# A pad of 384 bytes ahead of the SBUF tiles of a decode-attention kernel, so that rows loaded by DMA begin at multiples of 256 or 512 bytes

## Chip, cores, metric

One core of one Trainium2 chip. The time is device microseconds (us) of one execution. The kernel before takes 657.46 us (median of 5 runs, 657.27 to 658.13, which is 0.13%).

## The reference

One decode step of grouped-query attention with a large K and V cache, multiplied by a small MLP branch (the MLP is about 3 MB of weights and plays no part here). What matters is the size of the caches:

```python
B, Sq, D = 4, 1, 448
Hq, Hkv, Sk, Dh = 16, 8, 8192, 256          # k_cache, v_cache: (4, 8, 8192, 256) bf16
...
q = (xn @ wq)                                # one query row per batch and head
scores = einsum("bhqd,bhkd->bhqk", q, k) * Dh ** -0.5     # k, v repeated over 2 query heads
o = einsum("bhqk,bhkd->bhqd", softmax(scores), v)
s = o @ wo                                   # wo: (4096, 448)
return x + s * silu(mlp(xn))
```

There are 32 pairs (batch, kv head), here called heads. Each has 4 MB (4,096 KB) of K and as much of V, and each byte of them is read once. With the weights that makes 279 MB.

## The kernel before

All tiles are declared in one list, and they lie in SBUF in that order. Sizes are per partition:

```python
def sb(name, shape, dty):
    return es.enter_context(nc.sbuf_tensor(name, shape, dty))

kn = sb("kn", [P, 2, NCH, DH], BF16)         # 2 K slots of 32,768 B
vb = sb("vb", [P, 2, NCH, DH], BF16)         # 2 V slots of 32,768 B
kT = sb("kT", [P, RING, TB * P], BF16)       # 16,384 B
wo_sb = sb("wo_sb", [P, HQ, NHALF, D], BF16) # 16 rows of 1,792 B
...                                          # some 45 small tiles
```

In the built program 16,384 B of scratch and four constants of 32 B each lie ahead, so `kn` begins at byte 16,512 of each partition, `vb` at 82,048 and `wo_sb` at 163,968. Each of these is 128 B past a multiple of 256 (and of 512).

SP issues all large loads on one queue. Two K slots and two V slots are refilled as soon as compute has left them:

```python
def load_k(h):
    b, g = where(h)
    if h >= 2:
        sp.wait_ge(S["v_k"], h - 1)
    sp.dma_start(kn_dst(h), A_k_cache[b, g].rearrange("(p c) d -> p (c d)", p=P)
                 ).then_inc(S["dk%d" % (h % 2)], 16)
... # load_v alike; the last head's V in pieces
load_k(0)
load_k(1)
load_wo(NLATE, HQ, "dwo")                    # 12 rows of 1,792 B per partition
for h in range(2, NH):
    load_k(h)
    load_v(h - 2)
load_v(NH - 2)
load_v(NH - 1)
... # four late rows of wo
```

For each head PE transposes K (into PSUM), DVE and ACT copy it to `kT`, PE computes the scores, ACT the exponentials, and PE multiplies by V two heads later.

## Time and profile before

| | before |
|---|---|
| time, median of 5 runs | 657.46 us |
| span of the profiled run | 656.9 us |
| bytes moved by DMA | 279.13 MB |
| share of the span in which the main queue's packets occupy the 16 engines | 99.2% |
| PE idle, waiting for K, before the transposes | 76 us |

The page of the kernel before. The first two lines cut the span into 40 equal slices: how busy the DMA engines were, in tenths, and what they moved. Then come the totals and the DMA queues (packets, megabytes, share of 16 engines), and two issue lines (output<-source, count, KB each, median us from issue to landing):

```profile
...
DMA  8999999999999999999999999999999999999996
GB/s 360 440 413 425 434 427 437 425 439 427 437 427 435 429 435 431 431 435 427 437 429 433 429 433 429 433 429 433 429 435 431 433 431 435 429 433 433 429 425 256
DMA packets 12353, 279.13 MB, mean 425 GB/s; under 512 B 1204, under 2 KB 3256, under 8 KB 3768
## 3 DMA queue, kind: packets, MB, share of 16 engines
q1 hardware_dynamic: 12328, 278.99, 99.2%
...
kn<-in_A_k_cache_dram SPq DMA_DIRECT2D x32, 4096.0 KB, 25.7
vb<-in_A_v_cache_dram SPq DMA_DIRECT2D x31, 4096.0 KB, 31.3
```

The DMA is at 9 in every slice but the first and the last. A load of 4,096 KB moves in 9.7 us (8 packets on each engine, 1213.5 ns each), yet takes 25.7 us from issue to landing, so each stands behind another one in the queue. Now the waits of the same kernel (engine, tile and line; who ended the wait; us in total, times, longest), and the groups of the transposes and of the two evictions (busy us, mean ns of one, idle before and what ended it):

```profile
...
PE pst L588 <- PEq L245: 76.3, 28, 4.6
```

```profile
...
L588 PE MATMUL pst<-ident_b,kn 128*128 128x128 bf16 x4096 | 347.3, 239 | 78.6 <-PEq L245 76.3
L295 ACT ACTIVATE kT<-pst 128x1024 bf16<-128x1024 bf16 x224 | 229.3, 1024 | 360.6 <-ACTq L245 359.5
...
L293 DVE COPY kT<-pst 128x1024 bf16<-128x1024 bf16 x288 | 197.5, 691 | 263.7 <-DVEq L245 263.7
```

The first line is PE idle while K has not landed: 76.3 us in 28 waits. The two evictions stand idle before their input for 263.7 us (DVE) and 360.6 us (ACT). Compute has slack in every head; the DMA has none. So a nanosecond saved per packet should be saved in the time.

**Packets.** The trace also holds one record per DMA packet: start, duration, bytes. It does not name the engine, but they can be strung into 16 chains in which one packet follows the other without a gap (8,037 of the 8,064 packets of 32 KB have a successor within 40 ns of their bytes / 27.2), and the distance from one start to the next in a chain is what a packet costs. (These distances are worked out from the records, not lines of the profile. They were taken over whole ranges of packets and are good to a few hundredths of a ns in the mean. The duration in a record is 3 to 4 ns longer than the distance: 1213 against 1209.4 ns, 239 against 235.3, 469 against 465.9.) Times in the records' own clock run some 11 us ahead of the span's.

| packets, before | bytes / 27.2 | mean distance, first 50 us | mean distance, later |
|---|---|---|---|
| 32,768 B (K, V) | 1204.7 ns | 1209.8 ns | 1213.5 ns |
| 12,544 B (w3) | 461.2 | 465.9 | - |
| 6,272 B (w4) | 230.6 | 235.3 | - |
| 1,792 B (wo) | 65.9 | 70.6 | 75.3 |

At the start a packet of any of these four sizes costs its bytes at 27.2 B per ns plus 4.7 ns, both fitted to the distances (1209.4 less 235.3 ns for 32,768 less 6,272 B is 27.2 B per ns; 1209.8 and not 1209.4 for 32 KB, because two of the 16 engines already pay more in that stretch). Later it costs more for both sizes that occur later in number: 4.1 ns at 32,768 B (1213.5 less 1209.4) and 4.7 at 1,792 B (75.3 less 70.6). The 75.3 ns are those of the early wo load from 52 us of the records' clock on; the wo rows at the very end took 72.8.

### The profile page before, as it was taken

How to read it: one execution, taken by the hardware profiler on the slowest of the kernel's cores; microseconds unless marked ns; L12 is line 12 of the kernel's file. 1: busy time of each engine (PE TensorE's matmuls, PEld its weight loads, DVE VectorE, ACT ScalarE, POOL GpSimd, SP SyncE). 2: the span in 40 equal slices, each digit the busy share in tenths (PEclk: the TensorE clock that was granted, in tenths of full speed). 3: DMA queues.
4: the chain of work that ended last, by engine and by line, in shares of the span. 5: the costliest groups of instructions: out<-in, count | busy, mean ns of one | idle time of the engine just before them, and what ended most of it. 6: DMA issues, size and time to landing. Idle time of an engine off the chain costs nothing. (4 is left out here: it accounts for less than half of the span.)

```text
span 656.9 us, 22864 instructions
## 1 busy us (share of the span) xinstructions
PE 556.3 (85%) x9937; PEld 476.3 (73%) x9937; DVE 276.5 (42%) x589; ACT 256.0 (39%) x364; POOL 13.4 (2%) x77
## 2 busy tenths in 40 slices
PE   1899997988888988888897888898888889888897
PEld 0487886876766887667787766798767678766775
DVE  7353554443443444434443443444334443433442
ACT  4144544442433443323444333444333344433340
POOL 2000000000000000000000000000000000000000
PEclk9698999887899878889987888988878987887998
DMA  8999999999999999999999999999999999999996
GB/s 360 440 413 425 434 427 437 425 439 427 437 427 435 429 435 431 431 435 427 437 429 433 429 433 429 433 429 433 429 435 431 433 431 435 429 433 433 429 425 256
DMA packets 12353, 279.13 MB, mean 425 GB/s; under 512 B 1204, under 2 KB 3256, under 8 KB 3768
## 3 DMA queue, kind: packets, MB, share of 16 engines
q1 hardware_dynamic: 12328, 278.99, 99.2%
q8 instruction: 7, 0.11, 0.1%
q14 instruction: 2, 0.02, 0.0%
q10 hardware_dynamic: 16, 0.01, 0.0%
HBM read 278.99 MB, written 0.00 MB: 425 GB/s over the span
## 5 line engine op out<-in xcount | busy, mean ns | idle before, releaser
L588 PE MATMUL pst<-ident_b,kn 128*128 128x128 bf16 x4096 | 347.3, 239 | 78.6 <-PEq L245 76.3
L295 ACT ACTIVATE kT<-pst 128x1024 bf16<-128x1024 bf16 x224 | 229.3, 1024 | 360.6 <-ACTq L245 359.5
L588 PEld LDWEIGHTS pst<-ident_b,kn 128*128 128x128 bf16 x4096 | 275.4, 108 | 84.3 <-issue 83.8
L293 DVE COPY kT<-pst 128x1024 bf16<-128x1024 bf16 x288 | 197.5, 691 | 263.7 <-DVEq L245 263.7
L600 PE MATMUL psc<-qc,kT 128*128 128x2 bf16 x4096 | 178.7, 165 | 0.0
L600 PEld LDWEIGHTS psc<-qc,kT 128*128 128x128 bf16 x4096 | 157.7, 98 | 28.5 <-issue 28.3
L639 PE MATMUL psv<-vb,pT 128*4 128x512 bf16 x1056 | 86.4, 378 | 0.3 <-issue 0.3
L618 PE MATMUL psm<-sel,po 128*128 128x2 f32 x272 | 36.8, 257 | 0.5 <-PEq L245 0.5
L618 PEld LDWEIGHTS psm<-sel,po 128*128 128x128 f32 x272 | 34.8, 197 | 0.9 <-issue 0.9
L639 PEld LDWEIGHTS psv<-vb,pT 128*4 128x4 bf16 x1056 | 22.3, 82 | 15.3 <-issue 0.8
L452 DVE TENSOR_REDUCE rmax<-psc 128x2 f32<-128x128 f32 x32 | 9.3, 292 | 48.8 <-DVEq L245 48.8
L470 DVE COPY po<-psv 128x512 f32<-128x512 f32 x34 | 23.5, 692 | 3.0 <-DVEq L245 2.3
L457 DVE TENSOR_REDUCE gmax<-psm 2x1 f32<-2x128 f32 x32 | 8.9, 279 | 34.7 <-DVEq L245 34.7
L317 ACT ACTIVATE pT<-psc,negb 128x64 bf16<-128x64 f32 x66 | 20.6, 331 | 5.4 <-ACTq L245 5.4
L612 PEld LDWEIGHTS psm<-diag,ones_f 2*128 2x128 f32 x66 | 14.1, 263 | 6.4 <-issue 5.4
L280 POOL COPY qc<-qT 128x4 bf16<-128x4 bf16 x32 | 5.9, 186 | 585.8 <-DVEq L469 568.6
L612 PE MATMUL psm<-diag,ones_f 2*128 2x2 f32 x66 | 16.8, 321 | 1.1 <-PEq L245 0.9
L317 ACT ACTIVATION_READ_ACCUMULATOR pT<-psc,negb 128x1 f32 x66 | 13.6, 206 | 0.0
L608 PEld LDWEIGHTS psm<-ident_f,rmax 128*2 128x2 f32 x32 | 2.6, 80 | 14.0 <-issue 14.0
L536 PE MATMUL pst<-ident_b,xn_b 4*128 4x4 bf16 x14 | 0.6, 161 | 13.6 <-DVE xn_b L365 8.9
L630 PE MATMUL psm<-rowsum,ones_f 128*128 128x2 f32 x64 | 11.6, 251 | 0.0
L536 PEld LDWEIGHTS pst<-ident_b,xn_b 4*128 4x128 bf16 x14 | 0.5, 100 | 13.6 <-issue 8.9
(101 smaller groups left out, 122.4 us busy)
## 6 DMA issues: line engine op xcount, KB each, us to landing
kn<-in_A_k_cache_dram SPq DMA_DIRECT2D x32, 4096.0 KB, 25.7
vb<-in_A_v_cache_dram SPq DMA_DIRECT2D x31, 4096.0 KB, 31.3
vb<-in_A_wq_dram SPq DMA_DIRECT2D x1, 3584.0 KB, 11.7
vb<-in_B_w_dram SPq DMA_DIRECT2D x2, 1568.0 KB, 16.6
wo_sb<-in_A_wo_dram SPq DMA_DIRECT2D x1, 2688.0 KB, 44.3
kn<-in_A_v_cache_dram SPq DMA_DIRECT2D x1, 2048.0 KB, 25.2
kn<-in_A_v_cache_dram SPq DMA_DIRECT2D x1, 1024.0 KB, 27.3
kn<-in_A_v_cache_dram SPq DMA_DIRECT2D x2, 512.0 KB, 28.5
```

The source lines that it names most:

```text
L293: engine.tensor_copy(dst, src).then_inc(S["v_ev"], 1)
L295: engine.activation(dst, src, ACT.Copy).then_inc(S["a_ev"], 1)
L317: ins = act.activation(pv_p[:, :, hh], sc[:, :, hh], ACT.Exp, bias=negb[:, s, hh:hh + 1], scale=SCALE, accum_out=rowsum[:, s, hh:hh + 1])
L452: v.tensor_reduce(rmax[:, :], psc[h % 2][:, 0:NCH * REP].rearrange("p (k h) -> p h k", h=REP), AX.X, ALU.max).then_inc(S["v_rmax"], 1)
L457: v.tensor_reduce(gmax[:, :], psm[0:REP, 0:P], AX.X, ALU.max).then_inc(S["v_s"], 1)
L470: v.tensor_copy(po[:, slot], psv[:, 0:CP * DH]).then_inc(S["v_po"], 1)
L588: ins = pe.transpose(dst[:, t * P:(t + 1) * P], kn[:, h % 2, GC * j + kl, half * P:(half + 1) * P], ident_b[:, :])
L600: ins = pe.matmul(psc[h % 2][:, kk * REP:(kk + 1) * REP], kT[:, j % RING, t * P:(t + 1) * P], qc[:, h % 2, half, :], start=(half == 0), st ...
L612: pe.matmul(psm[:, P:P + REP], ones_f[0:REP, :], diag[:, :], start=True, stop=True).then_inc(S["p_m2"], 1)
L618: ins = pe.matmul(dst(dh)[:, 0:width], po[:, slot, i * DH + dh:(i + 1) * DH:NHALF], sel[:, i, 0:width], start=(i == 0), stop=(i == CP - 1))
L630: pe.matmul(psm[:, P + REP:P + 2 * REP], ones_f[:, :], rowsum[:, h % 2, :], start=True, stop=True)
L639: ins = pe.matmul(psv[o:o + CP * REP, 0:CP * DH], pT[:, h % 2, kk * REP:(kk + CP) * REP], src[:, kk:kk + CP, :].rearrange("p c d -> p (c d)"),
```

## The change

Its intent: bring the starts of the rows that the DMA writes to multiples of 256 or 512 B. It adds a tile that nothing reads or writes. The whole diff:

```diff
     NWARM = 14
+    ROW_PAD = 192
...
+        align = sb("align", [P, ROW_PAD], BF16)
         kn = sb("kn", [P, 2, NCH, DH], BF16)
         vb = sb("vb", [P, 2, NCH, DH], BF16)
```

192 elements of bf16 are 384 B. `kn` moves to byte 16,896 (33 x 512), `vb` to 82,432 (161 x 512) and `wo_sb` to 164,352 (321 x 512). K and V rows are 32,768 B, so all of them begin at multiples of 512; wo rows are 1,792 B (7 x 256), so they begin at multiples of 256.

## The prediction

Parts are cut from it where marked, because no trace or run of this case shows what they say. One is an argument that put the 4.7 ns of every packet down to its start off the boundary: 697 packets x 4.7 ns, 3.3 us in all. "That reading" in the text is this one; the prediction itself dropped it. So the 3.3 us is not in the sum, which came to 656.6 us, 0.9 below the 657.46 of before, for the chance of 2 to 3 us.

> **What bounds the kernel now.** The DMA engines. The slice table shows DMA 9 (90% or more) in all but the first and last of 40 slices, at 413 to 440 GB/s; the queue table gives 278.99 MB and 99.2% of 16 engines' time on one queue. In the waits, PE idles 76 us of 657 before the K transposes, while a K load takes 25.7 us from issue to landing although its 4 MB move in 9.7 us: a load always stands queued behind another. Compute has slack in every head, the DMA none. After the last weight piece some 6 us remain (chain of waits: last output matmuls 2.42 us, two DVE steps of 0.4 us, the store).
>
> **What one packet costs.** From the packet records of the trace, followed engine by engine: at the start a 32,768 B packet takes 1209.4 ns, a 12,544 B one 465.9, a 6,272 B one 235.3, a 1,792 B one 70.6. All fit bytes / 27.2 B per ns plus 4.7 ns[...]. From about 51 us on, the mean rises to 1213.5 ns (fixed part 8.8) and for 1,792 B to 75.3 (9.4). With some 697 data packets per engine the fixed parts sum to about 6 us; the bytes take 641 us.
>
> **What the change does.** It adds no instruction, byte or packet. By the declarations the first tile begins 128 B past a multiple of 512; the pad brings K and V rows (32,768 B) to multiples of 512 and wo rows (1,792 B) to multiples of 256.[...]
>
> **Does this trace agree?** Only by half. 4.7 ns is the fixed part, but w4 argues against that reading: of its two runs per partition one lands 128 B off a 256 B boundary and the other on a multiple of 512, and all 256 packets took 239 ns in the record (235.3 ns apart). So I take the fixed 4.7 ns to be independent of alignment. I can't exclude that the extra 4 ns per packet after 51 us is an alignment cost under contention; removing it would give, by estimate, 500 x 4.1 = 2 us. Removing every fixed cost would give 6 us, under 1%. Engines should be indifferent: all tiles move by the same 384 B (transposes 219 ns median, DVE evictions 691, ACT 1024).
>
> **Prediction.** 656.6 us, 8 times in 10 between 654.0 and 658.0. Faster by over 2%: 1%; within 2%: 98%; slower by over 2%: 1%. The likeliest outcome is no measurable change; the centre is pulled down by the chance of 2 to 3 us.
>
> **What would show each step.** Packets and bytes unchanged. Spacing of 32 KB packets in steady state: 1213.5 ns if alignment does nothing, 1209.4 if the later extra is alignment; at the start 1204.7 if the fixed part is. The w4 packets, whose two runs swap alignment, still 235.3 ns. Steady slices near 431 GB/s, or 433 to 435. PE's wait before the K transposes near 76 us, unless loads get faster.
>
> **What would make it wrong.** Compute reads of SBUF colliding with DMA writes in a way that depends on the offset[...].

## The result

655.51 us (median of 5 runs, 654.8 to 655.92) against 657.46: 1.95 us less. The ratio is 0.9963, 95% interval 0.9951 to 0.9975. A ratio here is made from all fast runs of both kernels, so it is not quite the ratio of the medians quoted. That is well within 2%, but the interval excludes 1.

The lines of the page after that answer to those shown of before:

```profile
...
DMA  8999999999999999999999999999999999999996
GB/s 362 444 421 421 443 421 446 421 444 423 444 423 444 421 446 421 446 421 446 421 443 423 442 425 442 425 442 425 438 429 438 429 438 429 434 434 434 434 424 288
DMA packets 12354, 279.13 MB, mean 427 GB/s; under 512 B 1205, under 2 KB 3257, under 8 KB 3769
## 3 DMA queue, kind: packets, MB, share of 16 engines
q1 hardware_dynamic: 12328, 278.99, 99.3%
...
kn<-in_A_k_cache_dram SPq DMA_DIRECT2D x32, 4096.0 KB, 25.2
vb<-in_A_v_cache_dram SPq DMA_DIRECT2D x31, 4096.0 KB, 30.5
```

```profile
...
PE pst L590 <- PEq L247: 76.0, 28, 4.5
```

```profile
...
L590 PE MATMUL pst<-ident_b,kn 128*128 128x128 bf16 x4096 | 345.8, 238 | 77.8 <-PEq L247 76.0
L297 ACT ACTIVATE kT<-pst 128x1024 bf16<-128x1024 bf16 x224 | 229.5, 1025 | 357.6 <-ACTq L247 356.7
...
L295 DVE COPY kT<-pst 128x1024 bf16<-128x1024 bf16 x288 | 197.5, 692 | 260.9 <-DVEq L247 260.9
```

Packets and bytes are the same (one packet more is an instruction fetch, on a different queue: q14 has 3 instead of 2). The DMA is as full as before, the mean rate went from 425 to 427 GB/s, and a K load lands in 25.2 us instead of 25.7. PE's wait for K is unchanged (76.0 us), and the groups that work in every head changed by at most 3 ns per instruction. What changed is in the packets:

| mean distance of packets | before | after | less per engine, over the whole run |
|---|---|---|---|
| 32,768 B, 8,064 of them | 1213.34 ns | 1209.41 ns | 1.98 us |
| 1,792 B, 2,043 counted | 73.50 | 70.45 | 0.39 |
| 4,096, 8,192 and 16,384 B (last head's V) | - | each 3.3 to 4.0 ns less | 0.12 |
| 28,672, 12,544, 6,272 B (first weights) | - | unchanged | 0.00 |

The last column is the difference times the number of packets over 16 engines. It sums to 2.5 us, where the medians differ by 1.95 and the ratio says 2.4. After the change, 8,049 of 8,064 K and V packets have the same recorded duration, 1213 ns; before nearly all lay between 1213 and 1228, spread. So the whole gain is the later extra, which is gone, and the 4.7 ns that every packet costs from the start is still there.

The two profiled runs differ by 3.8 us in their spans (656.9 and 653.1), more than the timed runs do. Part of that is luck at the end. The chain that ended last, before and after, in order of time (start us, us, what):

```profile
...
651.61 2.42 PE pst L687 x24
```

```profile
...
648.76 1.52 PE pst L689 x24
```

The same 24 last matmuls took 2.42 us in one run and 1.52 in the other. A windows line gives the stretch, each engine's busy us and instructions (PE, weight loads, DVE, ACT, POOL), the granted clock, the DMA share and GB/s; before and after:

```profile
...
651.00:654.50 3.50, 2.52 (x29) 1.95 (x25) 0.59 (x3) 0.00 (x0) 0.00 (x0) 0.60 0.08 31
```

```profile
...
648.00:651.00 3.00, 2.04 (x42) 1.49 (x41) 0.84 (x3) 0.00 (x0) 0.00 (x0) 1.00 0.15 55
```

The granted clock was 0.60 in the first and 1.00 in the second. That 0.9 us goes with the clock and not with the change: in the profiled run of `wo_late`, an experiment below that has the tiles at the old addresses, the same 24 matmuls took 1.43 us at a granted clock of 1.00, and in that of `pad352`, again off the boundary, 2.44 at 0.51. The line of `wo_late`:

```profile
...
660.79 1.43 PE pst L687 x24
```

### The profile page after: what moved, and what is told of

Its sections match the earlier page's. It is cut to its first block, busy times and chain, and to the rows that moved or that the text cites. A ratio compares the mean times of both kernels' runs of the same rounds, so it can differ in the third digit from the quotient of the medians.

```text
span 653.1 us, 22864 instructions
## 1 busy us (share of the span) xinstructions
PE 552.8 (85%) x9937; PEld 473.5 (73%) x9937; DVE 276.1 (42%) x589; ACT 256.2 (39%) x364; POOL 13.5 (2%) x77
## 6 DMA issues: line engine op xcount, KB each, us to landing
kn<-in_A_k_cache_dram SPq DMA_DIRECT2D x32, 4096.0 KB, 25.2
vb<-in_A_v_cache_dram SPq DMA_DIRECT2D x31, 4096.0 KB, 30.5
```

## The experiments

Theory A: a packet whose SBUF start is not on a 256 B boundary pays for itself. Rivals, as they came up: 512 B is the boundary; the move itself matters; the cost grows with the bytes below the start; short packets, compute, or other engines start the extra.

Every kernel gave the correct result except `bare`, `engines`, `onset` and `mix`, which load only and return zeros. `src_off` reads shifted K, yet its result was still within the tolerance of the comparison. "Distance" is the mean distance of 32 KB packets, in the kernels between 130 and 640 us of the records' clock.

### pad256, pad128, pad352, pad160: other sizes of the pad

```diff
-    ROW_PAD = 192
+    ROW_PAD = 128      # pad256; 64 in pad128, 176 in pad352, 80 in pad160
```

> Pad of 256 B: every tile moves, but K, V and wo rows begin 128 B past a multiple of 256 again, as before. Theory A (start against the 256 B boundary): as before, late 32 KB packets 1213.5 ns apart, time ratio to before 0.999 to 1.001. Rival D (it is the move, or having a pad, whatever its size): 1209.4 ns and a ratio of 0.996 to 0.997.

> Pad of 128 B: K and V rows begin 256 B past a multiple of 512, wo rows at multiples of 256. Theory A (256 B is the boundary): 1209.4 ns, ratio 0.996 to 0.997. Rival B (512 B is the boundary): an extra remains for K and V, 1211 to 1213.5 ns, ratio 0.998 to 1.000.

In the next two, theory A is taken with a cost in proportion to the bytes below the start: 224 and 32 B where the kernel before has 128 B and 4.1 ns. A mechanism given for it, which no run shows, is cut.

> Pad of 352 B: rows begin 224 B past a multiple of 256. Theory A[...]: extra 7/4 of 4.1 ns, so about 1216.6 ns, ratio 1.002 to 1.004. Rival C (any start off the boundary costs the same): 1213.5 ns, ratio about 1.000.

> Pad of 160 B: rows begin 32 B past a multiple of 256. Theory A[...]: extra about 1 ns, 1210.4 ns, ratio about 0.997. Rival C (any start off the boundary costs the same): 1213.5 ns, ratio about 1.000.

| kernel | start past a multiple of 256 (of 512) | distance | median of 5 | ratio to before (95%) |
|---|---|---|---|---|
| before | 128 (128) | 1213.50 ns | 657.86 us (9 runs) | 1 |
| pad256 | 128 (384) | 1213.44 | 657.75 | 0.9998 (0.9985 to 1.0012) |
| pad128 | 0 (256) | 1209.42 | 655.32 | 0.9955 (0.9941 to 0.9968) |
| pad352 | 224 (480) | 1214.53 | 658.56 | 1.0008 (0.9994 to 1.0022) |
| pad160 | 32 (288) | 1214.53 | 658.3 | 1.0006 (0.9992 to 1.002) |

Of 256 and 512 B, 256 B is the boundary: pad128 gets all of the gain (1209.42 ns) with K and V at odd multiples of 256, so rival B falls, and pad256, which moves every tile but keeps the residue, gets none (1213.44 ns), so rival D falls. That the cost grows with the bytes below the start falls too: 224 B and 32 B past the boundary cost the same 5.1 ns (1214.53 less 1209.42), where one would have been seven times the other. Being off the boundary is what costs, with a small difference between 128 B (4.1 ns) and 32 or 224 B (5.1 ns). The time alone could not have told 32 and 128 apart; the packet records do.

### src_off: the reading side

```diff
+                at = (b * HKV + g) * SK * DH - (64 if h < NH - HKV else 0)
+                at = max(at, 0)
+                kf = A_k_cache.rearrange("b g s d -> (b g s d)")
-                sp.dma_start(kn_dst(h), A_k_cache[b, g].rearrange("(p c) d -> p (c d)", p=P)
+                sp.dma_start(kn_dst(h), kf[at:at + SK * DH].rearrange("(p n) -> p n", p=P)
```

> The kernel after the change, but K of heads 0 to 23 is read from 128 B earlier in DRAM (result wrong on purpose); heads 24 to 31 and all V are read from the boundary. If a start off 256 B costs on the reading side as well: K packets of heads 0 to 23 about 1213.5 ns or more, those of 24 to 31 1209.4 ns. If only the SBUF side counts: 1209.4 ns throughout.

1209.41 ns throughout, with K of heads 1 to 23 shifted as well as with heads 24 to 31 (head 0 is not shifted, because the address is held at 0), and 654.53 us in its single run. A start in DRAM 128 B off the boundary costs nothing that shows (1209.41 ns, as after the change); a start 128 B off in SBUF costs 4.1. (K loads alternate here with V loads that are on the boundary. The next run shows that such a mixture hides most of an extra, but on the SBUF side it still left 1209.95 ns; and `bare`, below, has six shifted loads in a row.)

### k_only: K on the boundary, V off it

```diff
         kn = sb("kn", [P, 2, NCH, DH], BF16)
+        gap = sb("gap", [P, 64], BF16)
         vb = sb("vb", [P, 2, NCH, DH], BF16)
```

> K rows at multiples of 512 as after the change, but a gap of 128 B between the K and V slots puts V (and wo) 128 B off the boundary, as before. Theory A (each misaligned packet pays for itself): K packets 1209.4 ns, V packets 1213.5 ns, half of the gain, ratio to before about 0.998. Rival E (misaligned packets put the engines into a state in which all packets pay): K packets too above 1209.4 ns, and more than half of the gain is lost.

Neither came. The mean over K and V was 1209.95 ns: not half of the extra but an eighth of it (0.54 of 4.1 ns). The median was 656.46 us (655.42 to 658.13), ratio 0.998 (0.9968 to 0.9993), which fits half of the gain as well as nearly all of it; the packets decide. Successive distances on one engine, from a V load (off the boundary) over a K load to a V load (a bar stands for the 4 B packet that ends a load):

```
V: 1209 1210 1209 1210 1209 1209 1216 1209 | K: 1209 1213 1210 1209 1210 1209 1209 1210 | V: 1209 1210 1209 1209 1210 1209 1213 1211 | K: 1216 1209 ...
```

In each V load the first six packets pay nothing, the next two begin to pay, and one or two packets into K it is over. So theory A as stated falls: a misaligned packet does not pay for itself at once. The distances behave as if a sum grew over misaligned packets (six free, the next two dearer by up to 7 ns) and shrank over aligned ones; what it is a sum of they do not show.

### wo_late: without the early run of short packets

```diff
-            load_wo(NLATE, HQ, "dwo")
             for h in range(2, NH):
                 load_k(h)
                 load_v(h - 2)
+            load_wo(NLATE, HQ, "dwo")
             load_v(NH - 2)
```

> The kernel before, without a pad, with the early wo load (the one with 1,792 B packets) moved behind the loads of all heads but the last two. Tells what starts the extra. Rival F (the run of many short packets starts it): K and V packets stay at 1209.4 ns until wo is loaded near the end, ratio 0.997. If something else starts it (compute, time, or the loads themselves): 1213.5 ns from about 51 us or a little later, ratio about 1.000.

The extra set in without wo: the mean distance per load rose from 1209.8 to 1213.2 ns between 65 and 114 us of the records' clock, engine by engine: ten of the 16 began to pay 38 to 48 packets after K2's load began, six within 15. Why those six were early is open; six instruction fetches of 16 KB lie between 41 and 79 us of that clock, but that they are the reason is not shown. Rival F falls. The time rose to 663.28 us (ratio 1.0079), for another reason: the wo load had filled a hole. K2 is issued at 42.7 us (before), when compute has left the first K slot, and without wo nothing is queued before that. Windows lines, columns as above; before and wo_late:

```profile
...
30.00:40.00 10.00, 10.00 (x189) 9.13 (x188) 4.29 (x8) 5.76 (x10) 0.00 (x0) 0.98 0.94 394
40.00:45.00 5.00, 5.00 (x109) 3.66 (x110) 2.39 (x5) 1.88 (x2) 0.00 (x0) 1.00 1.07 388
```

```profile
...
30.00:40.00 10.00, 10.00 (x185) 8.98 (x184) 4.11 (x7) 5.60 (x9) 0.00 (x0) 0.96 0.76 326
40.00:45.00 5.00, 5.00 (x114) 3.85 (x114) 2.53 (x7) 2.05 (x2) 0.00 (x0) 1.00 0.39 105
```

From 40 to 45 us the DMA moved 105 GB/s instead of 388, from 30 to 40 us 326 instead of 394: (394 - 326) x 10 + (388 - 105) x 5 is 2.1 MB less, at 427 GB/s by estimate 4.9 of the 5.4 us. (The profiled run of wo_late was its slowest, 666.64 us; the other five took 662.9 to 663.34.)

### bare: loads alone, many offsets in one run

All compute is taken out. SP issues 4 MB K loads into four slots, one after another, each waiting only for the load that last used its slot:

```python
PHASES = (("d128", 64, 0, 6), ("wo", 64, 0, 1), ("d128b", 64, 0, 6), ("d0", 0, 0, 6), ("d128c", 64, 0, 6),
          ("d32", 16, 0, 6), ("d64", 32, 0, 6), ("d224", 112, 0, 6), ("d0s128", 0, 64, 6),
          ("d128s128", 64, 64, 6), ("d0b", 0, 0, 6))       # name, SBUF offset, DRAM offset (elements), loads
```

> Only loads, no compute (result wrong on purpose): six 4 MB K loads each with the SBUF start 128 B off, then wo at 128 B off, then 128, 0, 128, 32, 64, 224 B off, then DRAM 128 B off with SBUF at 0 and at 128, then both at 0. Theory A (the extra is the DMA engines' own): after the onset the phases at 128 take 1213.5 ns, at 32 and 224 about 1214.6, at 0 1209.4. Rival G (it needs compute engines that use SBUF beside the DMA): 1209.4 ns in every phase. Rival F (short packets start it): 1209.4 in the first phase, 1213.5 in the one after wo.

| phase | distance per load, ns (pauses left out) |
|---|---|
| 128 B | 1209.6, then 1209.4 five times |
| wo, 128 B | (short packets) |
| 128 B | 1213.6, then 1213.3 to 1213.5 |
| 0 | 1210.1, then 1209.4 |
| 128 B | 1209.4 three times, 1209.7, 1212.6, 1213.5 |
| 32 B | 1214.3 to 1214.8 |
| 64 B | 1213.3 to 1213.7 |
| 224 B | 1215.2, then 1214.4 to 1214.8 |
| 0, DRAM 128 B off | 1209.6, then 1209.4 |
| 128 B, DRAM 128 B off | 1209.4 three times, 1209.6, 1213.1, 1213.3 |
| 0 | 1209.8, then 1209.4 |

A windows line of this run shows how empty the compute engines are; the columns are as above, for DVE and POOL, the only ones that have work in it:

```profile
...
100.00:300.00 200.00, 0.00 (x0) 0.00 (x0) 1.00 1.00 433
```

No engine ran a single instruction in 200 us and the extra has the same size as in the kernel (1213.3 to 1213.5 ns against 1213.50; aligned 1209.4 in both), so rival G falls. Misaligned loads after aligned ones are free for about four loads (1209.4 to 1209.7 ns), with or without a DRAM offset, and pay from then on (1212.6 to 1213.5). After the short packets the next phase pays at once (1213.6 ns), as it would if each packet, short or long, counted alike; but six free loads came before them too, so this phase doesn't prove that they hastened it.

### engines: is it contention among DMA engines?

```python
PHASES = ((128, 16, 4), (17, 16, 5), (128, 16, 2), (34, 16, 4), (128, 16, 2), (68, 16, 3), (119, 16, 3), (128, 16, 3), (17, 0, 2))
# rows, SBUF offset in elements (32 B), loads; all loads of a phase have landed before the next begins
```

> Only loads of 32 KB rows, SBUF start 32 B past a multiple of 256[...], by numbers of rows that share the work among different numbers of DMA engines: 128 rows (16 engines), 17 rows (1 engine), 128, 34 rows (2), 128, 68 rows (4), 119 rows (7), 128; last 17 rows from the boundary. The phases are kept apart by waits. Theory H (the extra is an engine's own[...]): 1 engine alone also about 1214.5 ns. Rival I (the extra is contention among engines whose starts are off the boundary): 1 engine alone 1209.4 ns as if aligned, and the extra grows with the number of engines up to 1214.5 with 16.

The numbers of engines are those planned; the one of 17 rows can be read off its packets, which followed each other in one chain. Its distances, load by load, for the five loads 32 B off the boundary:

```
2363 1243 1209 1210 1209 1209 1210 1209 1210 1209 1209 1210 1209 1210 1209 1209 1210 |
1209 1210 1209 1209 1210 1209 1210 1209 1209 1210 1209 1210 1209 1217 1212 1213 1213 |
1218 1212 1213 1220 1213 1212 1213 1220 1213 1213 1213 1220 1213 1213 1213 1220 1213 |
1210 1220 1213 1213 1213 1220 1213 1213 1213 1220 1213 1213 1213 1220 1213 1213 1213 |
1217 1212 1213 1220 1213 1213 1213 1220 1213 1213 1213 1220 1212 1213 1213 1220 1213
```

The first 30 or so packets are free (1209 and 1210 ns, but for the first two); then a pattern of 1213, 1213, 1213, 1220 sets in, with a mean of 1214.7 ns, much as with 16 engines (1214.5). The last phase, 17 rows on the boundary, stayed at 1209 and 1210 after its first three packets. Rival I falls: one engine at work alone shows the whole extra. In the phases of 34, 68 and 119 rows many packets took far longer (12 of 136, 115 of 204 and 241 of 357 recorded durations are over 1240 ns, the longest 3.8 us); why is open, and these phases tell nothing of this question.

### onset: how long misaligned loads stay free

```python
PHASES = ((128, 64, 30), (128, 0, 1), (128, 64, 6), (128, 0, 1), (128, 64, 12), (128, 0, 2))
```

> Only K loads at 128 B off, thirty in a row and no short packets, then one load at 0, six at 128, one at 0, twelve at 128, two at 0. If short packets are needed for the extra to start: 1209.4 ns throughout. If it also builds up by itself (as V in k_only and the third phase of bare suggest): it sets in after some 5 to 40 packets per engine, stays until the aligned load, which brings 1209.4 ns after its first packet, and comes back in the loads that follow.

The first four loads (32 packets per engine) took 1209.4 to 1209.6 ns, the fifth 1210.5, all later ones 1213.2 to 1213.7. The aligned load took 1209.7, the misaligned one behind it 1210.4, the next 1213.5; the second time 1210.1, 1210.1, 1213.3. So no short packets are needed; it builds up by itself, from the fifth load on. (In bare the first six loads were free, not four and a half; in the fourth each engine paused for some 70 ns, which at 4.1 ns per packet would make up for 17 packets more, enough for 48. That is an estimate and was not followed up.)

From these numbers theory J was made, before the next run. It is a count fitted to the distances and names no cause. Each misaligned packet adds 4.1 ns (1213.5 less 1209.4) to a sum, and its distance stays 1209.4. When the sum is at about 150 ns (an estimate: some 35 packets x 4.1; engine by engine the extra set in after 30 to 37) it is full, and the distance becomes 1213.5. An aligned packet takes some of it off: in onset one aligned load of 8 packets bought about 6.1 free ones ((1213.5 - 1210.4) / 4.1 x 8), so 6.1 x 4.1 / 8 = 3.1 ns per packet, an estimate too. With these two rates k_only adds up as well: V adds 8 x 4.1 = 33 ns, K takes off 8 x 3.1 = 25, and 8 ns remain in 16 packets, 0.5 ns each; 0.54 was measured.

### mix: theory J's arithmetic, predicted

```python
PHASES = ((128, 64, 8), (128, 0, 2), (128, 64, 6), (128, 0, 3), (128, 64, 7), (128, 0, 5), (128, 64, 9),
          (128, 0, 1), (128, 64, 2), (128, 0, 1), (128, 64, 2), (128, 0, 1), (128, 64, 2), (128, 0, 1), (128, 64, 2),
          (128, 64, 2), (0, 0, 0), (128, 64, 8), (128, 0, 1))    # (0, 0, 0): wait until all has landed
```

The text calls the sum of theory J the backlog. Its account of a cause, which no run shows, is cut; its rates are the 4.1 and 3.1 ns and the 150 ns above.

> Only K loads. Theory J (backlog):[...] After 8 misaligned loads (backlog full): after 2, 3, 5 aligned loads the next misaligned packets are free of the extra for 12, 18 and 30 packets per engine; alternating 1 aligned and 2 misaligned loads gives a mean of 1211.1 ns; after a full stop of the queue, about 35 free packets again. Rival K (an aligned packet just resets a state, after which some 6 packets are free): about 6 free packets after 2, 3 and 5 aligned loads alike, and none after the stop, which brings no aligned packet.

| after | distances of the next misaligned loads, ns | free packets, measured | theory J | rival K |
|---|---|---|---|---|
| 2 aligned loads | 1209.5, 1211.2, 1213.5 | 12 | 12 | 6 |
| 3 aligned loads | 1209.4, 1209.4, 1212.8, 1213.3 | 17 | 18 | 6 |
| 5 aligned loads | 1209.4 three times, 1211.4, 1213.3 | 28 | 30 | 6 |
| a full stop | 1209.4 to 1209.5 four times, 1210.6, 1213.3 | 38 | 35 | 0 |
| 1 aligned, 2 misaligned, in turn | mean of three 1211.1 to 1211.3 | - | mean 1211.1 | - |

Free packets measured: 8 for each free load, and 8 x (1213.5 - d) / 4.1 of the load in which it sets in at mean distance d. Theory J gave all five numbers before the run, to within three packets; rival K missed all four of its own. What lies behind the sum, the runs do not show. A start off the boundary in DRAM alone added nothing to it: 1209.41 ns in src_off, 1209.4 in bare.

## Why the prediction was right or wrong

The predicted time was 656.6 us, 654.0 to 658.0; measured 655.51. That the range held says little of the mechanism: 656.6 lies between the two outcomes that the prediction weighed (657.46 without a gain, some 655.5 with 2 us), and the range covers both. The packets decide.

- **Bound by DMA, compute with slack: right.** The time fell with the packet distances (2.5 us by packets, 1.95 by medians, 2.4 by the ratio), and no engine's work changed. In the other direction, pad352 and pad160 have 1.0 ns more per packet, some 0.5 us in all, and their medians came out 0.7 and 0.4 us higher, though neither is clear of the noise.
- **No instruction, byte or packet changes; engines indifferent: right**, by the groups and the DMA totals.
- **The fixed 4.7 ns is independent of alignment: right.** It is still 4.7 ns (1209.41 against 1204.7) with every row on the boundary. The argument that put it down to the start, 3.3 us in all, was rightly dropped.
- **"The likeliest outcome is no measurable change": wrong.** The branch that I could not exclude, "the extra 4 ns per packet after 51 us is an alignment cost", was the true one, and its estimate, 500 x 4.1 = 2 us, met the measured 1.95 us. I weighed it too low because of w4. Its packets, on the boundary and off it, took the same 235.3 ns, and I read that as alignment not mattering to a packet. But w4 was loaded at 25.7 to 30.5 us of the records' clock, before the extra came at about 51, and onset and engines show that misaligned packets are free at first (1209.4 to 1209.6 ns for some 30 packets of an engine). Evidence from the free stretch was carried to the other one.
- **"Under contention": wrong.** The extra needs no compute (bare, 1213.4 ns) and no second engine (engines, 1214.7 ns). It set in during the run of short wo packets, from 51 us on; on theory J because the sum was full by then, if every packet adds the same to it. That short packets add to it as long ones do was not tested by itself; wo_late (1213.2 ns) and onset (1213.2 to 1213.7) show that the extra comes without them too.
- **"PE's wait before the K transposes near 76 us, unless loads get faster":** loads did get faster and the wait stayed at 76.0. Loads and compute both moved earlier together, by 2 to 3 us in 650, and a wait of 76 us in 28 pieces is no measure for that.

## What to carry to other kernels

In a kernel bound by DMA, as this one, begin every SBUF row that a DMA writes at a multiple of 256 B. Here this cost 128 B of padding per partition (pad128, ratio 0.9955) and gave 0.4%; most of that was there already with K alone on the boundary and V off it (k_only, 0.54 of 4.1 ns left). Short rows gain more in proportion once the extra shows, since the cost is per packet (4.7 of 75 ns at 1,792 B against 4.1 of 1213 at 32 KB). And before taking "these two cost the same" from a trace, ask whether the difference could be hidden in that stretch, as it was here for the first 30 to 38 misaligned packets of 32 KB of each engine (onset, engines, mix): look at a long, steady run of the same thing.
